# A one-column GpSimd copy ahead of each chunk's weight sums, and a shared tile for the fourth block of gate and up

## The chip, the core and the metric

The kernel runs on one core of one Trainium2 chip. The metric is device time in microseconds (us), the time of one execution of the whole program. Three executions of the kernel before gave 1979.97, 1982.2 and 1985.33 us; their median is 1982.2 us.

The engines are named as in the profile: PE is the matrix engine (PEld its weight loads), DVE is VectorE, ACT is ScalarE, POOL is GpSimd (the code and the diff call it Pool too), SP issues the DMAs. Each engine works through its own instructions in the order in which the program lists them, and waits on semaphores for the others.

## The reference, cut to what matters

```python
x = A_x                                             # 2048 rows of 512, float32
x = x + _A_ref(_layernorm(x), wq, wk, wv, wo, beta)   # 32 heads, 4 segments, memory carried along
x = x + _B_ref(_layernorm(x), w_gate, w_up, w_down)
x = x + _A_ref(...)                                 # the same two once more
x = x + _B_ref(...)

def _B_ref(x, w_gate, w_up, w_down):                # 512 -> 1792 -> 512
    g = _silu(x @ w_gate)
    u = x @ w_up
    return (g * u) @ w_down
```

Attention (`_A_ref`) isn't touched by the change. What follows speaks of `_B_ref`, which runs twice, once in each of two layers.

## The kernel before

**Numbers.** A float32 operand of a matmul is split in two: a high part (ACT rounds it to the matmul's type) and a low part (what is left, by a subtraction on DVE or POOL). A product is three matmuls for each piece of the contraction: high by high, low weight by high, high weight by low.

**Tiling of `_B_ref`** (function `ffn`). The 2048 rows are four blocks of 512, taken as two halves of two blocks (`m` = 0 and 1). The 1792 hidden columns are seven chunks of 256 (`c` = 0 to 6). Chunk 0 is computed directly (`up`). For chunks 1 to 6 gate and up are each a 2x2 product of blocks (two row blocks by two column blocks of 128), computed by `strassen` with seven block products in place of eight. That makes six such chunks in each half, two halves, two layers: 24 chunks.

The seven products need sums of the weight blocks and of the input blocks:

- `make_t` makes the four sums of the input once for each half (the tiles `TT`), on DVE.
- `load_s(c, "g")` and `load_s(c, "u")` fetch the weights of a chunk into two of four raw tiles (`phik_0`, `phik_1`, `phiq_0`, `phiq_1`), form four sums of 128x256 on POOL (helper `ew`, line L858, into the tiles `mem_0` and `mem_1`), round the high parts on ACT (L871) and subtract the low parts on POOL (L872: one of 128x256, three of 128x512).
- `load_d` fetches the chunk's rows of `w_down`, high part on ACT (L823), low part on POOL when its last argument is true (L825).

In `strassen` the products of gate land in the banks `plt_0` to `plt_2`, those of up in `ppv`, `pmx_0` and `pmx_1`; the matmuls are L996. DVE adds them up (helper `add`, L1009), each time one operand from a bank and one from a tile. The four result blocks of gate are in `tt_0`, `tt_1`, `of` and `raw`; those of up in `Y`, `xn_2`, `xn_3` and `pc`. ACT applies silu to gate's blocks in place (L949).

`finish` then takes each of the four blocks: DVE multiplies gate by up (L952, both operands are tiles in SBUF), ACT rounds the high part of the product into the hidden tile (L954, the names `vt` in the trace), DVE subtracts the low part (L955, again two tiles in SBUF). That is eight DVE instructions a chunk. The last of them writes the low part of block (0, 1), at the end of `hts[1]`. `down` multiplies the hidden tile by `w_down` (L1040) and DVE adds the result to the residual (L1045).

**What sets the order.** The kernel records operations first, with a priority made of a due time (`at(...)`) and a planned cost, and the tiles they read and write. `Program.issue` then plays a list scheduler over five engines and emits the instructions in the order in which they come out. So an edit can move instructions far from it. The semaphore waits of the emitted program come from what the instructions read and write. A dependency that is added by hand to an operation's `deps` is seen by the planner alone: it shifts the operation's place in its engine's order, and makes no engine wait. In the kernel before there is one such line in `ew`:

```python
                gp(0.65, lambda: getattr(nc.gpsimd, f)(out(), x(), y()), reads, [w_])
                P.ops[-1].deps |= set(after)
```

`after` is `done`, the last subtraction of the chunk before, and it is given to `load_s(c, "u", done)` alone. The high and low parts of `load_s` carry no such entry.

**Around a chunk's end.** In time the piece looks like this: PE ends the last products of up, and goes on at once with the first products of the next chunk's gate; DVE at that time does the last adds of up and the eight instructions of `finish`; behind them in DVE's order stand the first two adds of the next gate, `tt<-plt,tt`. The second writing of the bank `plt_1` on PE waits for the first of these adds. POOL at that time has the work of `load_s` for the next up.

Of the kernel before, what the change touches and what calls it, by code (L numbers as in the profile page):

```python
# [245 lines left out]
def infini_swiglu(ctx: ExitStack, tc: tile.TileContext, x, wq, wk, wv, wo, beta, wg, wu, wd, out,  # L246
# [11 lines left out]
    def sb(tag, shape, dtype=F32, ring=1):  # L258
        return P.buf(pool, tag, shape, dtype, ring)
# [12 lines left out]
    def dve(n, fn, reads, writes, fast=1):  # L272
        op("dve", n / 960 / fast + 0.0687, fn, reads, writes)

    def gp(cost, fn, reads, writes):
        op("pool", cost, fn, reads, writes)
# [528 lines left out]
    def ffn(base, x_in, x_out, slots, T):  # L805
# [40 lines left out]
        def load_s(c, nm, after=()):  # L846
# [17 lines left out]
            for wt, o0, o1, src, read in ((a, 0, 1, lambda: v0()[:, :, 0:128].rearrange("p k (o f) -> p o k f", o=1), r0),  # L864
                                          (a, 1, 3, lambda: m[0].ap, m[0]),
                                          (b, 0, 2, lambda: v1().rearrange("p k (o f) -> p o k f", o=2), r1),
                                          (b, 2, 4, lambda: m[1].ap, m[1])):
                n = 256 * (o1 - o0)
                hi = lambda wt=wt, o0=o0, o1=o1: wt.ap[:, o0:o1, 0]
                lo = lambda wt=wt, o0=o0, o1=o1: wt.ap[:, o0:o1, 1]  # L870
                act(n, lambda hi=hi, src=src: nc.scalar.copy(hi(), src()), [read], [(wt, (o0, 0))], sbuf=True)  # L871
                gp(n / 400, lambda hi=hi, lo=lo, src=src: nc.gpsimd.tensor_sub(lo(), src(), hi().bitcast(F32)),  # L872
                   [read, (wt, (o0, 0))], [(wt, (o0, 1))])

# [105 lines left out]
        def strassen(c, nm, m):  # L980
# [4 lines left out]
            C = {}  # L985
            for e, t in zip(((0, 0), (0, 1), (1, 0), (1, 1)),
                            ("tt_0", "tt_1", "of", "raw") if nm == "g" else ("Y", "xn_2", "xn_3", "pc")):
                C[e] = sb(t, [128, 2 if t == "pc" else 1, 512])

# [17 lines left out]
            def add(out, x, y):  # L1007
                v = lambda b: b.ap[:, 0] if b in C.values() else b.ap
                dve(512, lambda: nc.vector.tensor_add(v(out), v(x), v(y)), [x, y], [out])  # L1009
            prod(PX, a, 0, blk(h0, l0, 0))  # L1010
            act(512, lambda: nc.scalar.copy(C[0, 0].ap[:, 0], PX.ap), [PX], [C[0, 0]])
            prod(PY, a, 1, tk(1))
            add(C[0, 1], PY, C[0, 0])
            prod(PZ, b, 0, blk(h0, l0, 1))
            add(C[0, 0], PZ, C[0, 0])
            prod(PY, b, 2, tk(2))
            add(C[1, 0], PY, C[0, 1])
            prod(PX, a, 2, tk(0))
            add(C[1, 1], PX, C[1, 0])
            add(C[0, 1], PX, C[0, 1])  # L1020
            prod(PZ, b, 1, tk(3))
            add(C[1, 0], PZ, C[1, 0])
            prod(PY, b, 3, blk(h1, l1, 1))
            add(C[0, 1], PY, C[0, 1])
            order = ((0, 0), (1, 1), (1, 0), (0, 1))
            if nm == "g":
                for e in order:
                    gate(C[e], lambda e=e: C[e].ap[:, 0], lambda e=e: C[e].ap[:, 0], C[e])
            return C
# [46 lines left out]
        load_x(1)  # L1076
        for m in range(2):
# [24 lines left out]
            done = []  # L1102
            for c in range(1, NF):
                v = m * PAIR + 2 + (c - 1) * STEP
                at(v)
                sgs = strassen(c, "g", m)
                at(v + 0.25)
                load_s(c, "u", done)
                if c + 1 < NF:
                    at(v + 0.55)  # L1110
                    load_s(c + 1, "g")
                at(v + 0.8)
                load_d(c, RAW, True)
                end = m == 1 and c == NF - 1 and not isinstance(x_out, Buf)
                before = hts
                for part in ("ud" if end else "du"):
# [4 lines left out]
                    else:  # L1121
                        hts = {b: sb(slots[f"X{b}"], [128, 4 * 512], F32R) if end else hbuf(1 - b) for b in range(2)}
                        cs_ = strassen(c, "u", m)
                        at(v + FIN)
                        for e in ((0, 0), (1, 1), (1, 0), (0, 1)):
                            finish(sgs[e], lambda e=e, sgs=sgs: sgs[e].ap[:, 0], hts[e[1]], e[0],
                                   lambda e=e, cs_=cs_: cs_[e].ap[:, 0], cs_[e])
                        done = P.ops[-1:]
# [62 lines left out]
```

## Time and profile before

| What | Value |
|---|---|
| Median of three executions | 1982.2 us |
| Profiled execution: time | 1982.03 us |
| Profiled execution: span from first to last instruction | 1980.1 us |
| DVE busy | 1445.2 us (73%) |
| ACT busy | 865.5 us (44%) |
| Granted clock of PE, mean | 0.99 |
| `_B_ref` of layer 1 with its change-overs, about | 500 to 1000 us |
| `_B_ref` of layer 2, about | 1480 to 1980 us |

A line of the groups reads: source line, engine, operation, out<-in by tile names, count, then busy time, mean duration of one in ns, idle time of the engine ahead of them and what ended it. A line of the timeline reads: start in us, duration in us, engine, line, operation and tiles, and in brackets the idle time of the engine ahead of it and who ended it. A line of the waits reads: who waited for whom, us in total, how many times, the longest. A line on one source line reads: minimum, median and maximum of the duration in ns, then the first and last start.

### The profile page before, as it was taken

Reading aid. Unit: us, or ns where it says so; the run is one execution under the profiler, and the core shown is the slowest. Engines: PE = TensorE matmul, PEld = TensorE weight load, DVE = VectorE, ACT = ScalarE, POOL = GpSimd, SP = SyncE. Lnnn points to the kernel's source line nnn. Section 1 sums busy time; section 2 is a strip of 40 time slices with the busy share of each in tenths; the row PEclk is TensorE's granted clock in tenths of the full one; section 3 lists DMA queues with packets and bytes.
Section 4 is the critical chain, followed back from the end, with each engine's and each line's share of the span. In section 5 each row is a group of like instructions: output and inputs, shape, how many; then the busy total and the mean of one; then the engine's idle time right before and its main releaser. Section 6 shows DMA issues by size and latency. Waiting matters only on the chain.

```text
span 1980.1 us, 32338 instructions
## 1 busy us (share of the span) xinstructions
PE 1883.4 (95%) x11104; PEld 1438.5 (73%) x11104; DVE 1445.2 (73%) x3834; ACT 865.5 (44%) x1634; POOL 941.3 (48%) x1163
## 2 busy tenths in 40 slices
PE   7999999999899999999989999999999999999998
PEld 5777677776677777777767777777766777767776
DVE  6877777778666768766758677777896776786766
ACT  4555555445433333323325555554554423333321
POOL 5333444335546545646334344443354656554651
PEclk8999999999999999999999999999999999999999
DMA  7444434455132122211264344453641312221111
GB/s 240 124 113 129 129 113 152 132 155 167 51 119 61 43 64 91 69 44 54 85 197 129 112 130 113 129 160 108 187 145 49 125 46 64 75 75 43 43 53 43
DMA packets 120819, 206.09 MB, mean 104 GB/s; under 512 B 14160, under 2 KB 43856, under 8 KB 120656
## 3 DMA queue, kind: packets, MB, share of 16 engines
q1 hardware_dynamic: 118608, 203.49, 33.9%
q8 instruction: 89, 1.46, 0.3%
q10 hardware_dynamic: 2048, 0.53, 0.1%
q14 instruction: 74, 0.61, 0.1%
HBM read 136.34 MB, written 67.11 MB: 103 GB/s over the span
## 4 chain that ended last, share of the span: by engine, by line
PE 50%; DVE 15%; issue 2%; POOL 2%; ACT 2%; DMA 2%; SPq 0%; DVEq 0%; ACTq 0%; POOLq 0%
PE pj L1040 14%; PE pj L282 8%; PE plt L996 6%; PE pmx L996 5%; PE pmx L531 4%; PE ppv L603 3%; DVE vt L955 3%; PE plt L575 3%; PE ppv L996 2%; DVE tt L952 2%; DVE xn L1009 2%; PE pj L968 1%; POOL s L872 1%; DMA ck<-scrk 1%; DVE tt L1009 1%
## 5 line engine op out<-in xcount | busy, mean ns | idle before, releaser
L538 DVE CUSTOM_DVE_ANT_0 junk<-pmx,amask 128x128 bf16<-128x128 f32 (+3 forms) x1024 | 458.9, 485 | 121.5 <-PE pmx L531 115.9
L282 PE MATMUL pj<-s,s 128*128 128x512 f32 x1416 | 484.5, 409 | 1.7 <-DVE s L1045 1.4
L1040 PE MATMUL pj<-s,vt 128*128 128x512 f32 x1296 | 413.9, 399 | 11.5 <-DVE s L1045 5.6
L581 ACT ACTIVATE s<-plt 128x512 f32<-128x512 f32 x512 | 284.4, 601 | 144.2 <-PE plt L575 135.3
L996 PE MATMUL plt<-s,s 128*128 128x512 f32 x1008 | 305.6, 404 | 36.6 <-DVE tt L1009 34.6
L531 PE MATMUL pmx<-ck,s 127*128 127x256 f32 (+2 forms) x1024 | 301.1, 349 | 17.7 <-DVE mx L538 9.7
L282 PEld LDWEIGHTS pj<-s,s 128*128 128x128 f32 x1416 | 262.8, 190 | 66.7 <-issue 24.5
L1040 PEld LDWEIGHTS pj<-s,vt 128*128 128x128 f32 x1296 | 244.9, 190 | 75.5 <-DVE s L1045 10.1
L1045 DVE TENSOR_TENSOR s<-s,pj 128x512 f32<-128x512 f32 x224 | 153.2, 685 | 146.7 <-PE pj L1040 146.6
L996 PEld LDWEIGHTS plt<-s,s 128*128 128x128 f32 x1008 | 191.8, 192 | 92.0 <-DVE tt L1009 44.0
L575 PE MATMUL plt<-s,ck 128*128 128x256 f32 x1280 | 242.0, 289 | 4.9 <-ACT s L581 2.5
L531 PEld LDWEIGHTS pmx<-ck,s 127*128 127x128 f32 x1024 | 179.6, 190 | 91.2 <-issue 26.0
L996 PE MATMUL pmx<-s,s 128*128 128x512 f32 x720 | 240.6, 395 | 1.1 <-DVE xn L1009 0.7
L575 PEld LDWEIGHTS plt<-s,ck 128*128 128x128 f32 x1280 | 211.8, 190 | 33.4 <-ACT s L581 9.7
L585 POOL TENSOR_SCALAR_AFFINE_SELECT s<-s 128x512 f32<-128x512 f32 x192 | 127.2, 666 | 187.8 <-ACT s L581 179.2
L996 PEld LDWEIGHTS pmx<-s,s 128*128 128x128 f32 x720 | 134.5, 188 | 33.5 <-DVE xn L1009 2.4
L872 POOL TENSOR_TENSOR s<-mem,s 128x512 fp32r<-128x512 f32 x96 | 130.8, 1371 | 36.4 <-ACT s L871 36.4
L603 PE MATMUL ppv<-s,vt 128*32 128x512 f32 (+2 forms) x1536 | 136.8, 458 | 0.0
L872 POOL TENSOR_TENSOR s<-phik,s 128x512 fp32r<-128x512 f32 (+1 forms) x48 | 57.1, 1190 | 151.2 <-ACT s L871 151.2
L469 POOL TENSOR_SCALAR s<-raw 128x512 fp32r<-128x512 f32 x64 | 39.8, 622 | 186.4 <-ACT raw L468 183.1
L872 POOL TENSOR_TENSOR s<-phiq,s 128x256 fp32r<-128x256 f32 (+1 forms) x48 | 53.9, 1122 | 142.6 <-ACT s L871 142.6
L996 PE MATMUL ppv<-s,s 128*128 128x512 f32 x288 | 111.3, 393 | 0.0
(193 smaller groups left out, 2904.5 us busy)
## 6 DMA issues: line engine op xcount, KB each, us to landing
s<-scrq SPq DMA_DIRECT2D x128, 192.0 KB, 3.5
ck<-scrk SPq DMA_DIRECT2D x128, 192.0 KB, 4.6
scrq<-s SPq DMA_DIRECT2D x32, 512.0 KB, 3.0
scrk<-s SPq DMA_DIRECT2D x32, 512.0 KB, 3.0
scrq<-s SPq DMA_DIRECT2D x32, 256.0 KB, 2.0
scrk<-s SPq DMA_DIRECT2D x32, 256.0 KB, 2.0
xin<-xmid SPq DMA_DIRECT2D x32, 256.0 KB, 2.7
s<-xmid SPq DMA_DIRECT2D x32, 256.0 KB, 5.3
```

The lines of the kernel that those rows point to most:

```text
L282: pe(n, passes, lambda: nc.tensor.matmul(view(ps.ap), lhsT=av(a.ap), rhs=bv(b.ap), start=start, stop=stop), [(a, rk[0]), (b, rk[1])], [ps])
L531: nc.tensor.matmul(ps.ap[:, a * 256:a * 256 + nk], lhsT=cq.ap[0:127, 2 * j + p, qt * 128:(qt + 1) * 128], rhs=ck.ap[0:127, p, 0:nk], start ...
L538: dve(w, lambda a=a, qt=qt, w=w, ps=ps, junk=junk: nc.vector.tensor_tensor_reduce(out=junk.ap[:, :w], in0=ps.ap[:, a * 256:a * 256 + w], i ...
L575: nc.tensor.matmul(ps.ap[:, 256 * p:256 * p + 256], lhsT=ck.ap[:, p, kt * 128:kt * 128 + 128], rhs=cq.ap.rearrange("r (j p) c -> r p j c", ...
L581: act(512, lambda: nc.scalar.activation(Pb.ap[:, x].rearrange("p i c -> p (i c)"), ps.ap, AF.Exp, scale=SCALE), [ps], [(Pb, x)], table="exp")
L585: gp(0.593, lambda: nc.gpsimd.affine_select(out=Pb.ap[:, x], in_=Pb.ap[:, x], pattern=[[0, 4], [1, 128]], compare_op=OP.is_ge, fill=0.0, b ...
L603: nc.tensor.matmul(ps.ap[32 * i:32 * i + 32, q0:q0 + w], lhsT=vt.ap[:, kt, VW * hd:VW * hd + 32], rhs=f_[sl].ap[:, b0:b0 + w // 128, idx], ...
L872: gp(n / 400, lambda hi=hi, lo=lo, src=src: nc.gpsimd.tensor_sub(lo(), src(), hi().bitcast(F32)), [read, (wt, (o0, 0))], [(wt, (o0, 1))])
L955: dve(512, lambda: nc.vector.tensor_sub(hv(1), sv(), hv(0).bitcast(F32)), [sg, (ht, (fi, 0))], [(ht, (fi, 1))])
L996: pe(512, 1, lambda i=i, kc=kc, x=x, buf=buf, view=view: nc.tensor.matmul(ps.ap, lhsT=w.ap[:, o, i, kc], rhs=view(buf.ap, kc), start=(x == 0),
L1040: pe(512, 1, lambda i=i, j=j, fi=fi, x=x, ps=ps, wt=wt, cs=cs: nc.tensor.matmul(ps.ap, lhsT=ht.ap[:, 0:2048].rearrange("p (f a c) -> p f a ...
L1045: dve(512, lambda ps=ps, t=t: nc.vector.tensor_add(xb.ap[:, t, :], xb.ap[:, t, :], ps.ap), [ps, (xb, t)], [(xb, t)])
```

## The change

A new helper `pool_turn` records a POOL copy of one column (128x1, float32) into a small tile `turn`. For chunks 2 to 6 of a half it reads the last column that `finish` of the chunk before writes (the last column of the low part of block (0, 1) in `hts[1]`). For chunk 1 of the second half it reads the last column of the low part of `TT[2]`, the last that `make_t` writes. Chunk 1 of the first half has none. That makes 22 copies.

The recorded copy is then entered by hand into the `deps` of the chunk's POOL work: of all sums and all low parts of `load_s(c, "u")` and `load_s(c + 1, "g")`, and of the last low part of `load_d(c)`. Since these are instructions of the same engine as the copy, an order behind it is also a wait for what the copy waits for.

Beside that, the fourth result block of gate and of up no longer lies in `raw` and `pc`: one tile `pc` of two halves is made once for each `_B_ref` (`two`), and gate uses the first half, up the second.

```diff
@@ load_s @@
                 gp(n / 400, lambda hi=hi, lo=lo, src=src: nc.gpsimd.tensor_sub(lo(), src(), hi().bitcast(F32)),
                    [read, (wt, (o0, 0))], [(wt, (o0, 1))])
+                P.ops[-1].deps |= set(after)
+
+        def pool_turn(view, read):
+
+            one = sb("turn", [128, 1], ring=2)
+            gp(0.1, lambda: nc.gpsimd.tensor_copy(one.ap, view().bitcast(F32)), [read], [one])
+            return P.ops[-1:]
...
@@ strassen @@
-            C = {}
-            for e, t in zip(((0, 0), (0, 1), (1, 0), (1, 1)),
-                            ("tt_0", "tt_1", "of", "raw") if nm == "g" else ("Y", "xn_2", "xn_3", "pc")):
-                C[e] = sb(t, [128, 2 if t == "pc" else 1, 512])
+            C, V = {}, {}
+            for e, t in zip(((0, 0), (0, 1), (1, 0)), ("tt_0", "tt_1", "of") if nm == "g" else ("Y", "xn_2", "xn_3")):
+                C[e] = sb(t, [128, 512]), None
+                V[e] = lambda e=e: C[e][0].ap
+            C[1, 1] = two[0], nm
+            V[1, 1] = lambda: two[0].ap[:, "gu".index(nm)]
...
@@ ffn, the loop over chunks @@
+        two = [sb("pc", [128, 2, 512])]
...
-            done = []
             for c in range(1, NF):
                 v = m * PAIR + 2 + (c - 1) * STEP
                 at(v)
-                sgs = strassen(c, "g", m)
+                gs = strassen(c, "g", m)
+                at(v + 0.2)
+                if c > 1:
+                    turn = pool_turn(lambda ht=hts[1]: ht.ap[:, 1023:1024], (hts[1], (0, 1)))
+                elif m == 0:
+                    turn = []
+                else:
+                    turn = pool_turn(lambda t=TT[2]: t.ap[:, 1, 3, 1, 127:128], (TT[2], (1, 1)))
                 at(v + 0.25)
-                load_s(c, "u", done)
+                load_s(c, "u", turn)
                 if c + 1 < NF:
                     at(v + 0.55)
-                    load_s(c + 1, "g")
+                    load_s(c + 1, "g", turn)
                 at(v + 0.8)
                 load_d(c, RAW, True)
+                P.ops[-1].deps |= set(turn)
...
-                        done = P.ops[-1:]
```

**What moves on POOL.** The first place is chunk 5 of the first half in layer 2, POOL's order from the last low part of the chunk before on. L858 are the sums, L872 and L825 the low parts; `phik` and `phiq` are raw weights, `s` the split weights. Before:

```order
L825 TENSOR_TENSOR s_18859<-phiq_18832,s_18859 128x512
L872 TENSOR_TENSOR s_18995<-phik_18885,s_18995 128x256
L872 TENSOR_TENSOR s_19023<-phik_18911,s_19023 128x2x256
L858 TENSOR_TENSOR mem_19051<-phik_18885,phik_18911 128x256
L858 TENSOR_TENSOR mem_19057<-phik_18885 128x256
L858 TENSOR_TENSOR mem_19051<-mem_19051,phik_18885 128x256
L858 TENSOR_TENSOR mem_19057<-phik_18911,mem_19051 128x256
L872 TENSOR_TENSOR s_18995<-mem_19051,s_18995 128x2x256
L872 TENSOR_TENSOR s_19023<-mem_19057,s_19023 128x2x256
```

The same place after the change (the lines of the code are shifted by it; L879 is the copy):

```order
L825 TENSOR_TENSOR s_18865<-phiq_18855,s_18865 128x512
L879 COPY turn_19047<-vt_19013 128x1
L858 TENSOR_TENSOR mem_19050<-phik_18896,phik_18919 128x256
L858 TENSOR_TENSOR mem_19057<-phik_18896 128x256
L858 TENSOR_TENSOR mem_19050<-mem_19050,phik_18896 128x256
L872 TENSOR_TENSOR s_18994<-phik_18896,s_18994 128x256
L858 TENSOR_TENSOR mem_19057<-phik_18919,mem_19050 128x256
L872 TENSOR_TENSOR s_18994<-mem_19050,s_18994 128x2x256
L872 TENSOR_TENSOR s_19020<-phik_18919,s_19020 128x2x256
L872 TENSOR_TENSOR s_19020<-mem_19057,s_19020 128x2x256
```

All eight POOL instructions of the next up now stand behind the copy, the two low parts that need no sum among them.

The second place is the last chunk of that half, chunk 6, again on POOL. There the low parts of `w_down` (L825) come early, since no further gate is loaded. Before:

```order
L825 TENSOR_TENSOR s_19213<-phik_19175,s_19213 128x512
L825 TENSOR_TENSOR s_19213<-phik_19185,s_19213 128x512
L872 TENSOR_TENSOR s_19249<-phiq_19130,s_19249 128x256
L872 TENSOR_TENSOR s_19277<-phiq_19156,s_19277 128x2x256
L858 TENSOR_TENSOR mem_19305<-phiq_19130,phiq_19156 128x256
```

After the change:

```order
L825 TENSOR_TENSOR s_19212<-phik_19185,s_19212 128x512
L879 COPY turn_19298<-vt_19264 128x1
L858 TENSOR_TENSOR mem_19301<-phiq_19141,phiq_19164 128x256
L858 TENSOR_TENSOR mem_19308<-phiq_19141 128x256
L858 TENSOR_TENSOR mem_19301<-mem_19301,phiq_19141 128x256
L872 TENSOR_TENSOR s_19245<-phiq_19141,s_19245 128x256
L858 TENSOR_TENSOR mem_19308<-phiq_19164,mem_19301 128x256
L872 TENSOR_TENSOR s_19245<-mem_19301,s_19245 128x2x256
L872 TENSOR_TENSOR s_19271<-phiq_19164,s_19271 128x2x256
L872 TENSOR_TENSOR s_19271<-mem_19308,s_19271 128x2x256
L825 TENSOR_TENSOR s_19212<-phik_19195,s_19212 128x512
```

The second L825 has moved from ahead of the chunk's end to behind it.

**What doesn't move on DVE.** The third place is DVE at the end of chunk 4 of the same half, the chunk whose end the copy of the first place waits for. Before:

```order
L952 TENSOR_TENSOR of<-of,xn_18984 128x512
L1009 TENSOR_TENSOR xn_18960<-pmx_18933,xn_18960 128x512
L955 TENSOR_TENSOR vt_19016<-raw,vt_19016 128x512
L952 TENSOR_TENSOR tt_18804<-tt_18804,xn_18960 128x512
L955 TENSOR_TENSOR vt_18987<-of,vt_18987 128x512
L955 TENSOR_TENSOR vt_19016<-tt_18804,vt_19016 128x512
L1009 TENSOR_TENSOR tt_19049<-plt_19019,tt_19033 128x512
L1009 TENSOR_TENSOR tt_19033<-plt_19031,tt_19033 128x512
```

After:

```order
L959 TENSOR_TENSOR of<-of,xn_18983 128x512
L1018 TENSOR_TENSOR xn_18959<-pmx_18928,xn_18959 128x512
L962 TENSOR_TENSOR vt_19013<-pc,vt_19013 128x512
L959 TENSOR_TENSOR tt_18800<-tt_18800,xn_18959 128x512
L962 TENSOR_TENSOR vt_18986<-of,vt_18986 128x512
L962 TENSOR_TENSOR vt_19013<-tt_18800,vt_19013 128x512
L1018 TENSOR_TENSOR tt_19045<-plt_19016,tt_19029 128x512
L1018 TENSOR_TENSOR tt_19029<-plt_19027,tt_19029 128x512
```

Only the name of the fourth block's tile differs. On PE too the inner chunks of a half keep their order. Around the start of `_B_ref` in layer 1, the change of halves and the change from layer 1 to layer 2 the planner interleaves the work of all engines anew.

More of the change, by code (lines that the diff above doesn't have):

```diff
@@ L1005, in tk, with add @@
                 return [(TT[k], lambda t, kc, j=j: t[:, j, :, kc], j) for j in range(2)]
-            def add(out, x, y):
-                v = lambda b: b.ap[:, 0] if b in C.values() else b.ap
-                dve(512, lambda: nc.vector.tensor_add(v(out), v(x), v(y)), [x, y], [out])
+            def add(e, x, y):
+                y = C[y], V[y]
+                dve(512, lambda: nc.vector.tensor_add(V[e](), x.ap, y[1]()), [x, y[0]], [C[e]])
             prod(PX, a, 0, blk(h0, l0, 0))
-            act(512, lambda: nc.scalar.copy(C[0, 0].ap[:, 0], PX.ap), [PX], [C[0, 0]])
+            act(512, lambda: nc.scalar.copy(V[0, 0](), PX.ap), [PX], [C[0, 0]])
             prod(PY, a, 1, tk(1))
-            add(C[0, 1], PY, C[0, 0])
+            add((0, 1), PY, (0, 0))
             prod(PZ, b, 0, blk(h0, l0, 1))
-            add(C[0, 0], PZ, C[0, 0])
+            add((0, 0), PZ, (0, 0))
             prod(PY, b, 2, tk(2))
-            add(C[1, 0], PY, C[0, 1])
+            add((1, 0), PY, (0, 1))
             prod(PX, a, 2, tk(0))
-            add(C[1, 1], PX, C[1, 0])
-            add(C[0, 1], PX, C[0, 1])
+            add((1, 1), PX, (1, 0))
+            add((0, 1), PX, (0, 1))
             prod(PZ, b, 1, tk(3))
-            add(C[1, 0], PZ, C[1, 0])
+            add((1, 0), PZ, (1, 0))
             prod(PY, b, 3, blk(h1, l1, 1))
-            add(C[0, 1], PY, C[0, 1])
+            add((0, 1), PY, (0, 1))
             order = ((0, 0), (1, 1), (1, 0), (0, 1))
@@ L1027, in strassen @@
                 for e in order:
-                    gate(C[e], lambda e=e: C[e].ap[:, 0], lambda e=e: C[e].ap[:, 0], C[e])
-            return C
+                    gate(C[e], V[e], V[e], C[e])
+            return C, V
         ndn = [0]
@@ L1122, in ffn @@
                         hts = {b: sb(slots[f"X{b}"], [128, 4 * 512], F32R) if end else hbuf(1 - b) for b in range(2)}
-                        cs_ = strassen(c, "u", m)
+                        us = strassen(c, "u", m)
                         at(v + FIN)
                         for e in ((0, 0), (1, 1), (1, 0), (0, 1)):
-                            finish(sgs[e], lambda e=e, sgs=sgs: sgs[e].ap[:, 0], hts[e[1]], e[0],
-                                   lambda e=e, cs_=cs_: cs_[e].ap[:, 0], cs_[e])
-                        done = P.ops[-1:]
+                            finish(gs[0][e], gs[1][e], hts[e[1]], e[0], us[1][e], us[0][e])
                 pend = (0, 1)
```

## The prediction

> **What bounds the kernel now.** I read the page's busy shares first, then who waits for whom on PE, then the chain that ended last, and at last the timeline of one chunk's end.
>
> ```profile
> PE 1883.4 (95%) x11104; PEld 1438.5 (73%) x11104; DVE 1445.2 (73%) x3834; ACT 865.5 (44%) x1634; POOL 941.3 (48%) x1163
> ...
> PE plt L996 <- DVE tt L1009: 34.6, 20, 2.5
> ...
> PE pj L1040 <- DVE s L1045: 5.6, 4, 4.0
> PE pj L373 <- POOL xn L365: 4.4, 2, 2.2
> PE pj L1040 <- ACT vt L954: 2.8, 1, 2.8
> ```
>
> PE is busy 95% of the span. An edit that leaves its matmuls alone can only win from its idle time. The largest single wait on PE is one kind: gate's products (`plt`, L996) wait for DVE's add `tt` (L1009), 34.6 us in 20 places, 1.73 us each on average, 2.5 at most. That is one for nearly every one of the 24 chunks. The chain of work shows what stands ahead of it:
>
> ```profile
> 1628.23 1.71 DVE tt L952
> 1629.94 2.31 DVE vt L955 x2
> 1633.08 3.04 PE plt L996 x12
> ...
> 1660.57 1.71 DVE tt L952
> 1662.28 2.31 DVE vt L955 x2
> 1665.42 3.06 PE plt L996 x12
> ```
>
> In each chunk the chain leaves PE for the last three instructions of `finish` and comes back to PE with gate's product; the same place returns 32.34 us later. So here, and only here, DVE sets PE's time. Now DVE at that place:
>
> ```profile
> 1658.67 0.69 DVE L952 TENSOR_TENSOR of<-of,xn 128x512 f32<-128x512 f32 x1
> 1659.28 0.69 DVE L1009 TENSOR_TENSOR xn<-pmx,xn 128x512 f32<-128x512 f32 x1
> 1659.88 0.69 DVE L955 TENSOR_TENSOR vt<-raw,vt 128x512 fp32r<-128x512 f32 x1
> 1660.47 1.80 DVE L952 TENSOR_TENSOR tt<-tt,xn 128x512 f32<-128x512 f32 x1
> 1662.20 1.23 DVE L955 TENSOR_TENSOR vt<-of,vt 128x512 fp32r<-128x512 f32 x1
> 1663.36 1.22 DVE L955 TENSOR_TENSOR vt<-tt,vt 128x512 fp32r<-128x512 f32 x1
> 1664.68 1.49 DVE L1009 TENSOR_TENSOR tt<-plt,tt 128x512 f32<-128x512 f32 x2
> ```
>
> The same instruction takes 0.69 us at first and 1.80 or 1.23 later. What differs is POOL beside it:
>
> ```profile
> 1656.80 0.75 POOL L872 TENSOR_TENSOR s<-phik,s 128x256 fp32r<-128x256 f32 x1 [9.40 <-ACT s L871]
> 1660.02 1.71 POOL L872 TENSOR_TENSOR s<-phik,s 128x512 fp32r<-128x512 f32 x1 [2.47 <-ACT s L871]
> 1661.69 1.19 POOL L858 TENSOR_TENSOR mem<-phik,phik 128x256 f32<-128x256 f32 x1
> 1662.84 1.19 POOL L858 TENSOR_TENSOR mem<-phik 128x256 f32<-128x256 f32 x1
> ```
>
> From 1660.02 on POOL works on the next up's weights, and from then on every DVE instruction of the kind tile-by-tile is slow, until the add at 1664.68 (one operand from a bank), which is fast again beside POOL. POOL is slowed too. That this is the rule and not this chunk alone:
>
> ```profile
> L952 DVE TENSOR_TENSOR tt<-tt,xn x24: 677/1788/1804, 586.4 to 1958.1; 128x512 f32<-128x512 f32 x24
> L955 DVE TENSOR_TENSOR vt<-of,vt x23: 675/1226/1230, 587.6 to 1935.1; 128x512 fp32r<-128x512 f32 x23
> L858 POOL TENSOR_TENSOR mem<-phik,phik x24: 733/753/1192, 495.2 to 1934.6; 128x256 f32<-128x256 f32 x24
> L872 POOL TENSOR_TENSOR s<-mem,s x96: 1274/1297/4210, 498.1 to 1941.6; 128x512 fp32r<-128x512 f32 x96
> L1009 DVE TENSOR_TENSOR tt<-plt,tt x96: 678/692/693, 559.4 to 1946.4; 128x512 f32<-128x512 f32 x96
> ```
>
> The median of `tt<-tt,xn` is 1788 ns with a minimum of 677, while 96 adds with a bank operand never took over 693.
>
> **What the change does, and what each part costs.**
>
> *The wait becomes real.* The planner's entry of before put the four sums behind the last subtraction in the plan, but POOL never waited for it, and in the rows above it starts them 2.9 us before that subtraction ends (1661.69 against 1663.36 + 1.22 = 1664.58). The two low parts without a sum (1656.80 and 1660.02) had no entry at all. The copy reads what the subtraction writes, so POOL must wait, and all eight instructions stand behind it in POOL's order. So DVE has `finish` to itself.
>
> *What DVE gains in a chunk.* The multiplication falls from 1.80 to 0.69 (1.11 less) and would end at 1661.16. ACT's rounding of it follows 0.04 us after its end and takes 0.62, by
>
> ```profile
> 1662.31 0.62 ACT L954 CAST vt<-tt 128x512 fp32r<-128x512 f32 x1 [1.37 <-DVE tt L952]
> ```
>
> so it ends at 1661.82. The subtraction of `of` runs meanwhile, to 1661.8. The last subtraction then starts at about 1661.95 (0.1 for the signal, my estimate from gaps of 0.04 to 0.13 in these rows) and ends at 1662.64 in place of 1664.58. That is 1.94 us earlier, not the full 2.18 of the three instructions.
>
> *What PE gains.* PE's rows there:
>
> ```profile
> 1663.49 0.40 PE L1040 MATMUL pj<-s,vt 128*128 128x512 f32 x1
> 1665.42 1.89 PE L996 MATMUL plt<-s,s 128*128 128x512 f32 x7 [1.54 <-DVE tt L1009]
> ```
>
> PE stood idle from 1663.88 to 1665.42. With the add starting at 1662.74 and ending at 1663.43 the bank is free 0.4 us before PE gets there. All 1.54 us go. Over the kernel the 20 waits are 34.6 us. A chunk like this one can give up to 1.94; the longest wait is 2.5, which would leave 0.6, but long waits have more to win, as at the end of chunk 5 of a half, where the chain has
>
> ```profile
> 1686.59 1.48 DVE tt L952
> ```
>
> for the first multiplication of `finish`, 0.8 us over the usual. The low part of `w_down` that stands last ahead of that `finish` in POOL's order is moved behind the copy as well. I leave 1.0 us in all for rests, and count 33.6 us.
>
> *The 22 copies.* The trace has no POOL copy of this shape. The nearest rows:
>
> ```profile
> L355 POOL TENSOR_SCALAR bmv<-bmv x64: 208/225/662, 4.7 to 1742.4; 128x1 f32<-128x1 f32 x64
> L1178 POOL MEMSET const-float32-0.0<- 128x1 f32 x1 | 0.1, 98 | 0.3 <-issue 0.3
> ```
>
> Between 0.1 and 0.66 us; I take 0.23, the median of the row that reads and writes a column. That is 22 x 0.23 = 5 us on POOL, hidden in POOL's idle time (9.40 us ahead of the chunk's first instruction, above). Uncovered it would be those 5 us.
>
> *The later weights.* The work behind the copy is late, and behind it the next up's products on PE. From the copy's end at about 1663.0: three sums of 0.75 and the low part of 0.75 that the first product needs, 3.0 us, so 1666.0; then a sum and three low parts of 1.30, 4.65 us, so 1670.7 for all eight. PE wants them from here on:
>
> ```profile
> 1673.19 0.40 PE L996 MATMUL ppv<-s,s 128*128 128x512 f32 x1
> ```
>
> or 1671.65 after the gain. The first product has 5.6 us to spare, the last 1.0 before up even begins. Behind these stand the eight of the next gate (7.6 us) and two low parts (2.6 us): POOL is done at 1681, and `finish` comes back at 1686.59 less the gain, 1685. So the cover holds, at no cost. The second raw tile comes free at 1669.4, after the third low part; SP's load of `w_down` into it stands behind that in SP's queue and takes 2.6 us to land:
>
> ```profile
> phiq<-in_B_w_down_dram SPq DMA_DIRECT2D x26, 256.0 KB, 2.6
> ```
>
> That gives 1669.4 + 2.6 = 1672.0 for a low part that POOL reaches at 1678. No cost either.
>
> *The shared tile.* Gate's fourth block moves from `raw` to `pc`, same sizes, same engines. Cost zero inside a chunk. At the first chunk it now waits for the last reader of `pc` in attention, a chunk's time earlier. Together with the reordering at the change-overs I bound it by the other waits quoted on top (5.6 + 4.4 + 2.8 = 12.8 us): they could all go, or come twice. I take 0, since no row favours a side.
>
> Sum, against the profiled execution's own 1982.03 us: 1982.0 - 33.6 = 1948.4 us. The median of the three runs is 0.2 us away from that execution, so no correction.
>
> [...]
>
> **Rivals.**
>
> 1. *The collision is only partly gone.* If a POOL instruction still runs into the multiplication at the end (1.11 of the 1.94 us), DVE gains 0.83 a chunk: 20 x 0.83 = 16.6, 1965.4 us. For it: the low part of the chunk before could still be under way when `finish` starts, as at 1686.59. Against it: POOL's 9.40 us of idle time ahead of the first such instruction. Were adds held up in their place, the seven adds of gate that stand beside POOL would lose some 0.5 us each, 3.5 us, and give back more than the 1.94: 1982 us. The 693 ns speak against that.
>
> 2. *The wait moves to up's weights: slower.* Its place is the first product of up on PE, waiting for POOL's first low part. It decides when that part is over 5.6 us later than worked out. POOL and ACT take turns here (sums, roundings, low parts), and POOL has waited long for ACT:
>
> ```profile
> POOL s L872 <- ACT s L871: 147.5, 39, 14.5
> ```
>
>    That is 147.5 us in 39 waits in layer 2 alone, 3.8 on average. Two such waits ahead of the first product, 7.6 us, are 2.0 us over, in each of 22 chunks: 1982.0 - 33.6 + 22 x 2.0 = 1992 us. Against it: the first low part needs one rounding alone, and POOL found that done at 1656.80, six us ahead of the copy.
>
> 3. *PE finds its next wait in the same place*, for example for the second add or for the hidden tile's low part: 1980 us. Against it: the second add ends 0.7 us after the first, and the row at 1665.42 has seven matmuls without a wait for it.
>
> 4. *The change doesn't bind*: the copy's wait is met by something earlier and POOL goes on as before, 1982 us. Against it: the read column is the last one that the last subtraction writes.
>
> **How the numbers follow.** Forecast 0.74, rival 1 0.13, rival 2 0.05, rivals 3 and 4 0.05, and 0.03 for a larger gain at the change-overs. The forecast's own spread is the 12.8 us of the change-overs, of which I hold half likely on either side: 1942 to 1955. Rival 1 lies from 1955 to 1972, so the range goes to 1962, and holds 0.8. About 0.3% (6 us) is what a measurement of this kernel can tell from no change. Faster by more: 0.74 + 0.13 + 0.03 = 0.90; within: 0.05; slower: 0.05.
>
> **What would show it.** In the changed profile the wait of `plt` for `tt` falls from 34.6 us to under 3; the median of `tt<-tt,xn` falls from 1788 to about 690 ns, that of `vt<-of,vt` from 1226 to about 690; no L858 or L872 starts between the first multiplication and the last subtraction of a chunk; a chunk returns after about 30.8 us in place of 32.34; PE waits nowhere new at `ppv`. The forecast is wrong if `ppv` waits for POOL, if DVE's medians stay above 1 us, or if the change-overs lose more than 7 us.

## The result and the profile after

The changed kernel takes 1933.5 us (median of 4 runs, 1933.0 to 1937.6), the kernel before in the same session 1981.1 (1979.4 to 1985.3). The ratio is 0.9761 with a 95% interval of 0.9740 to 0.9782. That is 47.6 us less, where 33.6 were predicted; the time lies below the predicted range.

The page of the changed kernel, its first line and the busy times:

```profile
span 1931.2 us, 32319 instructions
...
PE 1870.8 (97%) x11104; PEld 1437.2 (74%) x11104; DVE 1406.9 (73%) x3834; ACT 873.0 (45%) x1634; POOL 905.9 (47%) x1185
```

PE is busy 12.6 us less than before, with the same 11104 matmuls. That could not come from shorter waits alone, and is the first sign that the prediction's account lacked something. Its waits (engine, tile and line, what it waited for: us in total, times, longest):

```profile
PE pj L282 <- DVE s L1054: 4.5, 2, 3.2
...
PE pj L373 <- POOL xn L365: 2.4, 2, 1.2
PE pmx L1005 <- ACT s L871: 2.4, 2, 2.1
PE plt L1005 <- ACT tt L1020: 2.3, 1, 2.3
...
PE plt L1005 <- DVE tt L1018: 0.4, 1, 0.4
```

The lines are shifted by the change (L996 is now L1005, L1009 is L1018). The 34.6 us of `plt` waiting for DVE's adds are 0.4. The third and fourth rows are new; both lie at the change of halves. The groups of `finish` (minimum, median and maximum in ns) and of the new copy:

```profile
L959 DVE TENSOR_TENSOR tt<-tt,xn x24: 675/682/685, 586.6 to 1909.2; 128x512 f32<-128x512 f32 x24
...
L962 DVE TENSOR_TENSOR vt<-of,vt x23: 677/683/1092, 587.8 to 1888.5; 128x512 fp32r<-128x512 f32 x23
...
L879 POOL COPY turn<-vt x20: 183/183/187, 589.1 to 1890.0; 128x1 f32<-128x1 f32 x20
L879 POOL COPY turn<-s x2: 1787/1788/1788, 773.2 to 1725.7; 128x1 f32<-128x1 f32 x2
```

The medians of 1788 and 1226 ns are 682 and 683. At the end of the same chunk as in the prediction, DVE's rows:

```profile
1629.48 0.68 DVE L962 TENSOR_TENSOR vt<-pc,vt 128x512 fp32r<-128x512 f32 x1
1630.08 0.68 DVE L959 TENSOR_TENSOR tt<-tt,xn 128x512 f32<-128x512 f32 x1
1630.68 0.68 DVE L962 TENSOR_TENSOR vt<-of,vt 128x512 fp32r<-128x512 f32 x1
1631.45 0.69 DVE L962 TENSOR_TENSOR vt<-tt,vt 128x512 fp32r<-128x512 f32 x1
1632.24 1.49 DVE L1018 TENSOR_TENSOR tt<-plt,tt 128x512 f32<-128x512 f32 x2
```

and POOL's:

```profile
1632.20 0.18 POOL L879 COPY turn<-vt 128x1 f32<-128x1 f32 x1 [13.32 <-DVE vt L962]
1632.34 0.74 POOL L858 TENSOR_TENSOR mem<-phik,phik 128x256 f32<-128x256 f32 x1
1633.04 0.75 POOL L858 TENSOR_TENSOR mem<-phik 128x256 f32<-128x256 f32 x1
```

From the start of the last multiplication to the end of the last subtraction DVE takes 2.06 us (1630.08 to 1632.14), before 4.11 (1660.47 to 1664.58). POOL starts its sums when that is over. The chain of work no longer leaves PE at this place:

```profile
1628.62 4.17 PE plt L1005 x18
1633.48 2.79 PE plt L1005 x12
...
1659.11 4.17 PE plt L1005 x18
1663.97 2.78 PE plt L1005 x12
```

The place returns after 30.49 us (1633.48 to 1663.97), before after 32.34: 1.85 us less, where the wait shown was 1.54.

### The profile page after: what moved, and what is told of

The parts are those of the page before. It is cut to its first block, busy times and chain, and to the rows that moved or that the text cites. A ratio compares the mean times of both kernels' runs of the same rounds, so it can differ in the third digit from the quotient of the medians.

```text
span 1931.2 us, 32319 instructions
## 1 busy us (share of the span) xinstructions
PE 1870.8 (97%) x11104; PEld 1437.2 (74%) x11104; DVE 1406.9 (73%) x3834; ACT 873.0 (45%) x1634; POOL 905.9 (47%) x1185
## 4 chain that ended last, share of the span: by engine, by line
PE 78%; DVE 8%; issue 4%; DMA 4%; POOL 3%; ACT 2%; SPq 0%; ACTq 0%; DVEq 0%; POOLq 0%
PE pj L282 16%; PE pj L1049 14%; PE plt L1005 11%; PE pmx L531 8%; PE pmx L1005 8%; PE ppv L603 7%; PE plt L575 6%; PE ppv L1005 3%; DVE junk L538 2%; DMA ck<-scrk 1%; PE pj L975 1%; PE pj L373 1%; PE pj L653 1%; DMA s<-nm 1%; POOL mem L858 1%
## 5 line engine op out<-in xcount | busy, mean ns | idle before, releaser
L1005 PE MATMUL plt<-s,s 128*128 128x512 f32 x1008 | 296.2, 396 | 3.4 <-ACT tt L1020 2.3
L1054 DVE TENSOR_TENSOR s<-s,pj 128x512 f32<-128x512 f32 x224 | 152.9, 684 | 137.9 <-PE pj L1049 137.7
L1005 PE MATMUL pmx<-s,s 128*128 128x512 f32 x720 | 239.2, 396 | 3.6 <-ACT s L871 2.4
L1005 PEld LDWEIGHTS plt<-s,s 128*128 128x128 f32 x1008 | 189.6, 189 | 50.4 <-ACT tt L1020 2.7
L1005 PEld LDWEIGHTS pmx<-s,s 128*128 128x128 f32 x720 | 135.5, 189 | 36.4 <-ACT s L871 3.2
L872 POOL TENSOR_TENSOR s<-mem,s 128x512 fp32r<-128x512 f32 x96 | 126.4, 1318 | 0.0
L1005 PE MATMUL ppv<-s,s 128*128 128x512 f32 x288 | 112.8, 394 | 0.0
L879 POOL COPY turn<-vt 128x1 f32<-128x1 f32 x20 | 3.7, 184 | 230.0 <-DVE vt L962 230.0
L581 ACT ACTIVATE pc<-plt 128x512 f32<-128x512 f32 x128 | 76.8, 600 | 63.8 <-PE plt L575 62.5
```

Source lines behind the costliest of these rows:

```text
L581: act(512, lambda: nc.scalar.activation(Pb.ap[:, x].rearrange("p i c -> p (i c)"), ps.ap, AF.Exp, scale=SCALE), [ps], [(Pb, x)], table="exp")
L1005: pe(512, 1, lambda i=i, kc=kc, x=x, buf=buf, view=view: nc.tensor.matmul(ps.ap, lhsT=w.ap[:, o, i, kc], rhs=view(buf.ap, kc), start=(x == 0),
L1054: dve(512, lambda ps=ps, t=t: nc.vector.tensor_add(xb.ap[:, t, :], xb.ap[:, t, :], ps.ap), [ps, (xb, t)], [(xb, t)])
```

## The experiments

Two questions are open. Why is the gain some 13 us larger than the waits that went (47.6 us against 34.6 less 0.4)? And is it POOL's wait for VectorE that brings it, as the prediction had it? All ratios are to the kernel before, with 95% intervals; "a chunk" is the distance from the first multiplication of the `finish` of chunk 4 to that of chunk 5, in the first half of layer 2.

| run | median us | ratio, interval | a chunk, us |
|---|---|---|---|
| before (profiled) | 1982.0 | 1 | 32.4 |
| changed kernel | 1933.5 | 0.9761, 0.9740 to 0.9782 | 30.5 |
| after2 (the same, again) | 1936.0 | 0.9759, 0.9745 to 0.9772 | 30.5 |
| e3_order | 1938.4 | 0.9780, 0.9763 to 0.9797 | 30.5 |
| e3_again | 1936.0 | 0.9763, 0.9748 to 0.9778 | 30.5 |
| e8_low | 1950.9 | 0.9836, 0.9807 to 0.9865 | 30.5 |
| e7_deps | 1946.4 | 0.9817, 0.9793 to 0.9841 | 30.5 |
| e4_sums | 1952.9 | 0.9850, 0.9834 to 0.9867 | 31.4 |
| e1_tile | 1976.5 | 0.9984, 0.9966 to 1.0002 | 32.3 |
| e2_turn | 1940.2 | 0.9788, 0.9771 to 0.9805 | 30.5 |
| g2 | 1955.5 | 0.9865, 0.9848 to 0.9882 | 31.4 |
| g3 | 1969.7 | 0.9938, 0.9923 to 0.9952 | 32.2 |
| g4 | 2008.2 | 1.0122, 1.0103 to 1.0141 | 34.4 |
| e5_noTT | 1937.4 | 0.9773, 0.9753 to 0.9792 | 30.5 |
| h1_place | 1929.3 | 0.9726, 0.9713 to 0.9739 | 30.5 |

### The place in the order, without the wait

The copy becomes a fill that reads nothing. The planner still puts it behind VectorE's last low part, so that every engine has the order of the changed kernel, instruction for instruction, and only the wait is gone.

```diff
-        def pool_turn(view, read):
+        def pool_turn(done):
             one = sb("turn", [128, 1], ring=2)
-            gp(0.1, lambda: nc.gpsimd.tensor_copy(one.ap, view().bitcast(F32)), [read], [one])
+            gp(0.1, lambda: nc.gpsimd.memset(one.ap, 0.0), [], [one])
+            P.ops[-1].deps |= set(done)
             return P.ops[-1:]
```

> The changed kernel with the order of every instruction on every engine unchanged, but the 22 copies are fills of a constant, which read nothing and so wait for nothing: POOL has the place in the order, not the wait. Theory A (the wait does it): POOL's sums run beside the finish again, the muls and subs are back at 1.2 to 1.8 us, the 20 waits are back at 1.3 to 1.7 us each, 1970 to 1985 us. Theory C (the new order does it, on POOL or by another interleaving of down's matmuls): 1930 to 1945 us.

It took 1938.4 us: theory A fell. Once more, on one chip with the changed kernel:

> The changed kernel itself once more, beside the two others of this call: 1931 to 1937 us by every theory.

> The kernel with the fills in place of the copies (orders of the changed kernel, no wait) once more, on the same chip as the changed kernel, since its first run stood at 1938.4 us against theory A's 1970 to 1985. Theory E (the order takes the two low parts of the weights behind the sums, and that alone frees the finish in most chunks; the wait only adds the chunks where POOL comes late): 3 to 7 us over the changed kernel. Theory A after all (the first run was a mishap): over 1970 us.

Both medians are 1936.0 us. Under theory E a difference of 3 to 7 us was expected; there is none that stands clear of the noise (the first pair of ratios, 0.9780 and 0.9761, would be 3.8 us, with intervals that overlap). So in this order the wait, taken over the whole kernel, brings a few us at most, and nothing that these runs can show. POOL's rows in the run with the fills, then two of DVE's:

```profile
1622.44 2.56 POOL L825 TENSOR_TENSOR s<-phiq,s 128x512 fp32r<-128x512 f32 x2
1624.91 0.14 POOL L879 MEMSET turn<- 128x1 f32 x1
1624.96 0.78 POOL L858 TENSOR_TENSOR mem<-phik,phik 128x256 f32<-128x256 f32 x1
...
1626.35 0.78 POOL L858 TENSOR_TENSOR mem<-mem,phik 128x256 f32<-128x256 f32 x1
1633.33 0.74 POOL L872 TENSOR_TENSOR s<-phik,s 128x256 fp32r<-128x256 f32 x1 [6.20 <-ACT s L871]
1634.02 0.74 POOL L858 TENSOR_TENSOR mem<-phik,mem 128x256 f32<-128x256 f32 x1
```

```profile
1637.03 0.68 DVE L960 TENSOR_TENSOR tt<-tt,xn 128x512 f32<-128x512 f32 x1
1637.64 0.68 DVE L963 TENSOR_TENSOR vt<-of,vt 128x512 fp32r<-128x512 f32 x1
```

Three sums start ten us and more ahead of the last multiplication, the fourth and a low part 2.3 us ahead of it (1634.76 to 1637.03); POOL then waits for ACT until `finish` is over. So the sums come before its end, not behind it. In the kernel before they came late because in POOL's order they stood behind two low parts, of which the second (1660.02 in the prediction's rows) waited for ACT's rounding until `finish` was at its end. The new order puts the sums first, and POOL has been free for them all along.

It isn't free in every chunk. In the run with the fills, `finish` of chunk 1 still has the sums beside it (its three last subtractions take 1.2 us each), and the stretch from there to the next takes 34.9 and 35.2 us in place of 33.3 and 33.1. On the other side the change of halves (the last `finish` of one half to the first of the next) takes 67.7 and 65.8 us in place of 70.3 and 68.5. The two roughly even out (3.7 us against 5.3).

### The order alone, without any instruction

One line is added to the kernel before, in `load_s`, and nothing else:

```diff
                 gp(n / 400, lambda hi=hi, lo=lo, src=src: nc.gpsimd.tensor_sub(lo(), src(), hi().bitcast(F32)),
                    [read, (wt, (o0, 0))], [(wt, (o0, 1))])
+                P.ops[-1].deps |= set(after)
```

> The kernel before with one line more and no instruction more: the planner also ties the low parts of up's weights to the last low part of the chunk before, as it does their sums already, so that in POOL's queue the sums come ahead of the two low parts that stood before them. No copy, no fill, no shared tile, no wait. Theory E (those two low parts, of which the second waits for ACT's rounding until 5.8 us into the finish and held the sums until then, are the whole of it): 1932 to 1945 us, muls and subs at 0.7 us in most chunks. Rival F (the copy or fill as an instruction, the shared tile, or the ties of the next gate's weights and of down's are needed too): 1955 to 1982 us.

With all ties of the changed kernel, but still no copy, fill or tile (`done` in place of `turn` in `load_s` of the next gate and behind `load_d`):

> The kernel before with all the ties of the changed kernel in the planner (low parts of up's weights, sums and low parts of the next gate's, down's last low part), but neither copy, fill nor shared tile. Theory E: within 10 us of the run with the low parts' ties alone, 1930 to 1945 us. Rival F, if the instruction or the tile counts: 1955 to 1982 us.

In the chunks theory E holds to the letter. With the one line:

```profile
L953 DVE TENSOR_TENSOR tt<-tt,xn x24: 676/680/687, 588.2 to 1929.3; 128x512 f32<-128x512 f32 x24
...
L956 DVE TENSOR_TENSOR vt<-of,vt x23: 675/680/692, 589.4 to 1908.7; 128x512 fp32r<-128x512 f32 x23
```

and a chunk takes 30.5 us, as in the changed kernel. The whole times, 1950.9 and 1946.4, are above what it expected, by 6 and 1 us, and below what rival F did. What is missing against the changed kernel lies outside the steady chunks: with the one line the changes of halves take 73.6 and 76.3 us in place of 70.3 and 68.5, 11 us together (in the second of them PE waits 4.6 us for one add). With all ties they take 69.6 and 71.9. PE's order with the one line is that of the kernel before in the steady chunks, and another one around the start of `_B_ref` in layer 1 and the change-overs. So the instruction isn't needed for the chunks; for the change-overs the runs only show that they differ with every edit.

### The wait without the order of the low parts

The changed kernel, with the low parts of the weights and down's last low part no longer tied to the copy (the line with `deps` behind `tensor_sub` in `load_s` and the one behind `load_d` are taken out).

> The changed kernel with only the four weight sums tied to the copy; the low parts of the weights and the last low part of down's are free in the order again. Theory A: what stands behind the copy in POOL's queue waits all the same, what the order puts ahead of it runs beside the finish: low parts slow one or two of its muls, 1933 to 1955 us, with waits of up to 0.8 us each. Rival (the low parts collide as much as the sums): 1960 to 1980 us.

1952.9 us, at the upper end. POOL's rows at a chunk's end, then DVE's:

```profile
1641.05 1.71 POOL L872 TENSOR_TENSOR s<-phik,s 128x512 fp32r<-128x512 f32 x1 [2.47 <-ACT s L871]
1644.75 0.18 POOL L878 COPY turn<-vt 128x1 f32<-128x1 f32 x1 [1.99 <-DVE vt L961]
1644.89 0.72 POOL L858 TENSOR_TENSOR mem<-phik,phik 128x256 f32<-128x256 f32 x1
```

```profile
1641.51 1.79 DVE L958 TENSOR_TENSOR tt<-tt,xn 128x512 f32<-128x512 f32 x1
1643.23 0.68 DVE L961 TENSOR_TENSOR vt<-of,vt 128x512 fp32r<-128x512 f32 x1
1644.00 0.69 DVE L961 TENSOR_TENSOR vt<-tt,vt 128x512 fp32r<-128x512 f32 x1
```

The two subtractions are free of the sums, the multiplication is still slowed by the low part ahead of the copy. A chunk takes 31.4 us, half-way. So in the old order the wait does win something: about 1 us a chunk. With the runs above this makes a table of four: low parts ahead of the sums and no wait 32.4, with the wait 31.4; sums ahead and no wait 30.5, with the wait 30.5.

### Each half of the change alone

The shared tile without copy and ties; then copy and ties with the tiles of before:

> Only the shared tile for the fourth block of gate and up; no copy on POOL, and the sums' order tied to the last low part of the chunk before as in the kernel before. Theory A (all of the gain comes from POOL's waiting for VectorE's last low part): no change against before, 1976 to 1986 us, and the 20 waits of the plt matmuls for the adds stay near 1.5 us each. Theory B (the tile, or the order that the planner makes with it, gives the 14 us that the prediction missed): 1963 to 1971 us.

> Only the copy on POOL with what hangs on it; the fourth blocks of gate and up have the tiles of before. Theory A: the time of the changed kernel, 1930 to 1938 us. Theory B: 1943 to 1952 us, the 14 us stay away.

The tile alone leaves the 20 waits at 34.6 us and changes nothing that can be told from no change. The copy alone has all of the gain but some 5 us (0.9788 against 0.9761 and 0.9759), and even these are at the edge of the noise, since the intervals just touch. Its trace has one wait that the changed kernel has not:

```profile
970.71 0.50 PE L1050 MATMUL pj<-s,vt 128*128 128x512 f32 x1 [4.17 <-ACT vt L961]
```

It lies at the change of layers, behind the fourth block (`raw`) of the last `finish` of layer 1. So the tile is probably worth about this wait, through the order that the planner finds there; this was not tried by itself.

### What a wait of PE costs

To price a wait by itself, the changed kernel gets 2, 3 or 4 idle copies on VectorE ahead of gate's first add in 20 chunks, right behind the last subtraction. No order changes.

```diff
-            def add(e, x, y):
+            def add(e, x, y, n=0):
                 y = C[y], V[y]
-                dve(512, lambda: nc.vector.tensor_add(V[e](), x.ap, y[1]()), [x, y[0]], [C[e]])
+
+                def fn():
+                    for _ in range(n):
+                        nc.vector.tensor_copy(junk[0].ap, x.ap)
+                    nc.vector.tensor_add(V[e](), x.ap, y[1]())
+                dve(512, fn, [x, y[0]], [C[e]] + junk[:n])
...
-            add((0, 1), PY, (0, 0))
+            add((0, 1), PY, (0, 0), 2 if nm == "g" and c > 1 else 0)
```

> The changed kernel, every order unchanged, with two idle copies (128x512 out of PSUM) on VectorE ahead of the gate's first add in 20 chunks, so right after the last low part: a delay of some 1.2 to 1.4 us (estimate from the adds' 0.69 us), to be read from the trace. Theory A (the delay counts whole, because a wait of PE also empties its pipeline: the period grew by 1.9 us where the wait shown was 1.54): 20 x 1.3 = 26 us more than the changed kernel, 1956 to 1964 us, no loss of clock. Theory D (a wait costs its shown idle time, the delay less 0.4 us): 18 us more, 1949 to 1954 us.

> As with two copies, with three: a delay of 1.8 to 2.1 us, about that of the slowed finish before (1.94 us). Theory A: 20 x 1.95 = 39 us and some losses of the clock (1.7 us each, 3 to 6 of them) more than the changed kernel, 1970 to 1984 us. Theory D: 20 x 1.55 = 31 us more, 1960 to 1967 us.

> As with two copies, with four: a delay of 2.4 to 2.8 us, waits of 2.0 to 2.4 us. Theory A with the clock: 20 x 2.6 = 52 us and the clock at half for 3.4 us behind most of the waits (15 to 20 x 1.7 = 25 to 34 us), 2005 to 2022 us. Theory A without the clock (a wait costs the same whether over or under 2 us): 1982 to 1989 us. Theory D: 1975 to 1981 us.

A copy delays by 0.62 us: with three, gate's first add starts 2.66 us after the last subtraction started (1659.85 to 1662.51), in the changed kernel 0.79 (1631.45 to 1632.24). The waits of `plt` for the adds in the three runs are, of two, of three and of four copies, 14.9, 29.4 and 43.9 us in 20 places each. The table sets out where the time went, against the changed kernel. "Idle" is the span less PE's busy time on the page, "clock" the span times one less the mean granted clock, here with the four digits that the traces keep. The run with the tied sums alone (e4_sums) is added, since it too has 20 waits.

| | span | idle | clock | rest | `plt` waits |
|---|---|---|---|---|---|
| changed kernel | 1931.2 | 60.4 | 12.5 (0.9935) | | 0.4 |
| two copies | +23.2 | +17.0 | -0.4 (0.9938) | +6.6 | 14.9 |
| three | +40.0 | +31.1 | +3.0 (0.9921) | +5.9 | 29.4 |
| four | +74.8 | +42.9 | +28.8 (0.9794) | +3.1 | 43.9 |
| kernel before | +48.9 | +36.3 | +6.7 (0.9903) | +5.9 | 34.6 |
| tied sums alone | +20.2 | +17.8 | -2.3 (0.9948) | +4.7 | 15.3 |

So a wait cost more than its length here, in two ways. The first is a piece of about 0.3 us for each wait (6.6 us in 20 waits of the run with two copies, where the clock plays no part; only with four copies the rest is smaller, 3.1 us, and why is open). By the ratios two copies cost some 21 us, between theory D's 18 and A's 26; three cost some 35, between D's 31 and A's 39; four some 72, and their 2008.2 us lie where A with the clock expected them. So neither theory has the price of a short wait right: it is the shown wait and a piece on top. PE's rows around the wait in the kernel before show it:

```profile
1663.26 0.39 PE L996 MATMUL plt<-s,s 128*128 128x512 f32 x1
1663.49 0.40 PE L1040 MATMUL pj<-s,vt 128*128 128x512 f32 x1
1665.42 3.06 PE L996 MATMUL plt<-s,s 128*128 128x512 f32 x12 [1.54 <-DVE tt L1009]
1668.32 0.39 PE L1040 MATMUL pj<-s,vt 128*128 128x512 f32 x1
```

In a stream a matmul starts every 0.23 us (1663.26 to 1663.49), though each is shown 0.4 long. From 1663.49 to 1668.32 there are 13 starts to go, which make 2.99 us in a stream. They took 4.83: the wait cost 1.84 us, not the 1.54 shown. 0.17 us of it is the end of the last matmul, which the stream would have hidden (0.40 less 0.23). Most of the remainder is at the first matmul behind the wait: it's shown 0.50 us long, and the next one starts 0.34 us after it; from there on the distance is 0.23 again.

The second is the clock. In the kernel before, most of the 20 waits were 1.5 to 1.8 us, a few about 2.0 or more. Three of the latter:

```profile
653.69 4.62 PE L996 MATMUL plt<-s,s 128*128 128x512 f32 x12 [1.99 <-DVE tt L1009]
720.25 3.05 PE L996 MATMUL plt<-s,s 128*128 128x512 f32 x12 [2.04 <-DVE tt L1009]
1698.47 4.60 PE L996 MATMUL plt<-s,s 128*128 128x512 f32 x12 [2.08 <-DVE tt L1009]
```

Behind the third, twelve such matmuls take 1.54 us more than behind the wait of 1.54 us; behind the first it's the same, behind the second not, though its wait is longer than the first's. In the kernel before 4 of the 20 waits are like that, in the run with four copies 16 of 20; a row of its PE and the stretches of 2 us around it (PE, PEld, DVE, ACT and POOL busy, then the granted clock):

```profile
1649.90 4.60 PE L1005 MATMUL plt<-s,s 128*128 128x512 f32 x12 [2.09 <-DVE tt L1022]
```

```profile
1647.00:1649.00 2.00, 0.81 (x4) 0.33 (x2) 1.90 (x4) 0.00 (x0) 2.00 (x4) 1.00 0.00 0
1649.00:1651.00 2.00, 1.10 (x3) 0.92 (x4) 1.54 (x3) 0.33 (x1) 1.16 (x2) 0.82 0.24 27
1651.00:1653.00 2.00, 2.00 (x6) 1.57 (x5) 0.00 (x0) 1.64 (x4) 1.11 (x1) 0.50 0.28 104
1653.00:1655.00 2.00, 2.00 (x8) 1.58 (x8) 0.69 (x1) 0.00 (x0) 2.00 (x3) 0.83 0.01 4
```

The clock falls to 0.50 and 1.70 us are lost (2.00 x (0.18 + 0.50 + 0.17)), so it stands at 0.50 for 3.4 us. In the run with three copies, with waits of 1.3 to 1.7 us and one of 2.25, the clock fell behind one of the 20, a wait of 1.66 us. Against it, four copies are 0.6 us of delay more in 20 places, 12 us, and the span grew by 35 us.

### The change of halves

The two new waits of PE lie at chunk 1 of the second half, where the copy reads the low part of `TT[2]`. First PE's row, then POOL's, in the changed kernel:

```profile
1731.16 0.50 PE L1005 MATMUL pmx<-s,s 128*128 128x512 f32 x1 [2.09 <-ACT s L871]
```

```profile
1725.71 1.79 POOL L879 COPY turn<-s 128x1 f32<-128x1 f32 x1 [17.16 <-DVE s L941]
1727.46 0.73 POOL L858 TENSOR_TENSOR mem<-phiq,phiq 128x256 f32<-128x256 f32 x1
1728.15 1.18 POOL L858 TENSOR_TENSOR mem<-phiq 128x256 f32<-128x256 f32 x1
```

POOL waits 17 us for the last difference, and the sums and their roundings on ACT are late behind it. In layer 2 PE waits for such a rounding, in layer 1 for an ACT copy that stands behind one. The granted clock is 0.50 from 783.2 to 786.7 in layer 1 and from 1732.1 to 1735.6 in layer 2, 3.4 us each. First the two copies were taken out with all that hangs on them (`turn = []` for chunk 1 of the second half, as the first has it):

> The changed kernel without the two copies that read the low part of the third difference at the first chunk of the second half of each layer (20 copies stay). Theory A: the two waits of PE that are new there (2.09 us for ACT's rounding at 1729, 2.30 us for ACT's copy at 781, both followed by 3.4 us at half the clock, some 1.7 us each) go, 4 to 9 us less than the changed kernel, 1925 to 1930 us. Rival: the sums then run beside the making of the differences on VectorE again, as before, and the older waits at the change of halves come back in the place of these: 1931 to 1940 us.

That gave no gain (0.9773; theory A's 1925 to 1930 us fell). Without the ties the planner makes other orders there, and the changes of halves take 69.8 and 73.0 us: the rival, with the second longer than before the edit and than in the kernel before (70.4). Then the place was kept and only the wait taken away:

```diff
+        def pool_place(after):
+            one = sb("turn", [128, 1], ring=2)
+            gp(0.1, lambda: nc.gpsimd.memset(one.ap, 0.0), [], [one])
+            P.ops[-1].deps |= set(after)
+            return P.ops[-1:]
...
             make_t(m)
+            made = P.ops[-1:]
...
-                    turn = pool_turn(lambda t=TT[2]: t.ap[:, 1, 3, 1, 127:128], (TT[2], (1, 1)))
+                    turn = pool_place(made)
```

> The changed kernel with its 20 copies in the chunks, but the two copies of the third difference's low part replaced by fills that wait for nothing, every order unchanged. Theory E: the two new waits of PE at the change of halves (2.1 and 2.3 us with their 3.4 us at half the clock) go, as in the run with 22 fills, where the two stretches from the last finish of one half to the first of the next took 67.7 and 65.8 us in place of 70.3 and 68.5: 4 to 6 us less than the changed kernel, 1927 to 1931 us. Rival: what is gained there comes late again at the next chunk, within 2 us of the changed kernel.

1929.3 us, against 1936.0 for the changed kernel on the same chip; the intervals of the two ratios don't meet. It is the fastest version here. PE's waits for the sums' side at this place are now

```profile
PE plt L1012 <- ACT tt L1027: 1.2, 1, 1.2
...
PE pmx L1012 <- POOL s L872: 0.4, 1, 0.4
```

and the changes of halves take 67.5 and 65.8 us.

## Why the prediction was right and wrong

**What bounds it: right.** The 20 waits of `plt` were the thing to win, and slowed instructions of `finish` beside POOL were their cause. Where the slowing is gone in a run, the waits are gone with it but for rests (5.2 us in 6 places in the run with the fills, 6.6 in 7 with the one line, 4.6 of them at one change of halves).

**"The wait becomes real": a true statement, and not the reason.** POOL does wait now, and the prediction gave the free `finish` to that. The runs with fills and with the one line give DVE the same 0.68 us without any wait in most chunks. The reason is the sentence that the prediction put beside it: the two low parts "had no entry at all", and now stand behind the sums. It worked out when the sums would start behind the copy, and didn't ask when POOL would start them if they merely stood first. POOL's 9.40 us of idle time, quoted for another purpose, held the answer.

**The slowed rows: right.** In the prediction's rows POOL's subtraction at 1660.02 takes 1.71 us, where the median of that size is 1.30 (1297 ns, `s<-mem`). DVE's subtraction at 1659.88 started before it and runs until 1660.57. Counted from there, 1.30 us end at 1661.87, close to the 1661.73 shown; DVE's multiplication (1660.47) ends 0.54 us later, POOL's sum (1661.69) 0.61 us after that, and so on in turns. So in these rows the instructions of the two engines end by turns; why they do, no run tried by itself. The forecast didn't hang on the reason.

**What DVE gains: right.** 1.94 us a chunk predicted, 2.05 measured.

**What PE gains: the step that failed, in its size.** "All 1.54 us go. Over the kernel the 20 waits are 34.6 us", less 1.0 for rests. The rests were right (0.4 us stayed). But a wait was priced at its shown length, and what PE loses behind it stood at nothing, without a reason. Measured in the profiled spans, the idle time fell by 36.3 us, the lost clock by 6.7 (four waits at 1.7 us each), and 5.9 are the pieces on top of the waits: 48.9, for the 47.6 of the medians. The idle copies, with nothing else changed on PE, POOL and ACT, show the same prices. The rows `1665.42 3.06` against `1698.47 4.60` behind two such waits were in the trace of the kernel before.

**The copies: right for 20, wrong for two.** 0.18 us against 0.23 taken. The two at `TT[2]` take 1.79 us each, and their wait costs the 6.7 us that the run without it gained.

**The later weights, rival 2.** No wait at `ppv`, as worked out. At one place in each layer POOL did come late by the turn-taking with ACT, 2.3 us in layer 1 and 2.1 in layer 2, in two chunks and not in 22.

**Rival 1** is the run with the tied sums alone: the low part meets the multiplication in its chunks, which costs half of a chunk's gain. The rival's 1965 us came out as 1952.9: against the kernel before, 18.5 us of idle time went, close to its 16.6, and 9.0 us of lost clock besides, with waits left of at most 1.5 us (15.3 us in 20 places) and a mean clock of 0.9948 in place of 0.9903.

**The shared tile and the change-overs.** Zero inside a chunk was right. At the change of layers the tile seems worth about 5 us together with the copy, which the 12.8 us of bounds covered. PE's other waits fell by about 2 us in sum (36.3 less the 34.2 of the `plt` waits), against 0 taken.

## What to carry to other kernels

Where an engine's order is made by a planner, an edit that adds a wait can change the order too. Test the place without the wait, by an instruction that depends on nothing, before crediting the wait: here the place alone gave the whole gain, and at two spots the wait was a loss. Price a wait of PE by what the stream loses (from start to start, counted in the steady interval) and by the clock behind it, not by the idle time in front.

## What the runs showed of the hardware

PE's clock fell behind some of its waits, and not always behind the longest. Of the 20 waits of `plt` for the adds it fell behind none with two copies (0.6 to 1.5 us), behind one with three (1.66 us; not behind 2.25), behind 4 in the kernel before (1.99, 2.08, 2.09 and 2.45 us; not behind 1.95 and 2.04) and behind 16 with four copies (2.05 to 2.96 us; not behind 2.09, 2.17 and two of 2.27). So the length alone doesn't decide it. What else does, no run shows. In the kernel before each of the four falls is to 0.50, lasts 3.41 us (the third from 1699.44 to 1702.85) and costs 1.7 us.

A POOL copy of one column took 0.183 us at `hts[1]` and 1.788 us at `TT[2]`, same shape, both times behind a long wait. The rows beside the slow ones point to the collision of `finish`: the one at 773.21 began while DVE worked on the first of three tile-by-tile instructions in a row, each at 0.68 us, and ended at 775.00, 0.05 us after the last of them; the one at 1725.71 ended at 1727.50, again 0.05 us after the last of three. In both places DVE's next instruction takes an operand from a bank (L1054). The quick copy at 1632.20 had an add with a bank operand beside it. It would be another form of it, since here POOL alone waits, for three instructions and not for one. No run tried this by itself.
